# Three warm-up products moved behind the modulation, and all engine orders of an adaLN block replaced by another plan

## The chip, the core and the metric

The kernel runs on one core of a Trainium2 chip. The metric is device time in microseconds (us). Before the change the runs gave 277.48 us in the median (277.21 to 277.81, three runs).

## The reference

One transformer block with adaptive layer norm, on 2048 tokens of width D = 448. A vector c gives six modulation vectors. The first half is causal attention over a sliding window of 256 tokens with 16 heads of width 28, the second a gated MLP whose gate mixes tokens by a 2048 x 2048 matrix.

```python
mod = (silu(c) @ w_mod).reshape(1, 6, 1, 448)
sa, ca, ga, sb, cb, gb = mod[:, 0], ..., mod[:, 5]
h = layernorm(x) * (1 + ca) + sa
x = x + ga * (window_attention(h @ wqkv) @ wo)
h = layernorm(x) * (1 + cb) + sb
z = gelu(h @ w_in)                     # 448 -> 2 * 896
z2 = layernorm(z[..., 896:])
g = w_sp @ z2 + b_sp                   # over the tokens
x = x + gb * ((z[..., :896] * g) @ w_out)
```

## The kernel before

**Order.** The kernel writes down 1180 operations, each with what it depends on; an operation is a short group of instructions on one engine. Which engine executes an operation that could go to several (a copy out of PSUM, a normalisation), in what order each engine takes its operations, and which PSUM bank or buffer each one uses is all read from one string, `PLAN`, at the top of the file. An entry `p71.0` is operation 71, on TensorE, in bank or buffer 0; the letters p, d, a, t, s stand for TensorE (PE), VectorE (DVE), ScalarE (ACT), GpSimd (POOL) and SyncE (SP, which issues most DMAs). A program derives the semaphore waits from the dependencies and from that order. Each engine, and SP's queue, takes its operations strictly in the order of the plan.

**Stages, with the lines that the prediction names.**

- Start. `wmodA` (the part of `w_mod` for sa and ca), `wq_st`, `wv` and x are loaded. 37 warm-up products of a constant tile (L513, made at L566, called fillers) keep PE busy: 27 are meant for the time ahead of the modulation, ten for the gaps behind it. c is transposed (L516), silu applied (L519), and four operations of eight narrow products (L547) make sa and ca from `wmodA`. Four token tiles are transposed on PE (L750) and modulated on the way out of PSUM (L759, L761) into `hT`, the transposed h.
- Attention works in blocks of 512 tokens, in tiles of 128. `WQK` holds the q and k weights with each head padded to 32 rows (L619, L620). Products give K (L836, copied out to `KT` at L848 and L849), q (L812 for the first block, L778 for the others; copied to `qT` at L787, L788, L817) and V (L856, copied to `Vaug` at L860, L861). Scores: L941 for the first tiles, L971 (48 matmuls for half a tile), and L982 for a narrow rest that uses `QBD`, a block diagonal copy of q (cleared at L523, filled at L806, L830). Then the exponential on ACT (L927), the causal and window mask by a multiplication on DVE (L990, L1010), the product with V (L1017), the division by the row sums (L1031, L1033), a DMA that transposes the result (L466), the product with `wo_g` (L1043), and the sum with x on DVE (L1047). `wo_g` is `wo` scaled by ga (`gg_sb`), in four pieces (L603).
- The layer norms of the later blocks take statistics on DVE (L634, L637), a small addition (L641), a power on POOL (L643), a product (L659), and the normalisation (L654, or L661 with the mean folded in); then a DMA transposes the tile into `hT` (L466), and `hT` is modulated in four pieces a block (L740 on ACT, L742 on DVE or POOL; L1066, L1068 in the second half).
- The MLP: products with `w_in` for z2 (L1141, two token tiles a group) and z1 (L1162, transposed, four pieces a group), gelu on ACT (L1148 and L1170), the norm of z2 (L634 to L643, then L1153 on DVE). When all 16 tiles of z2 are normalised, the spatial product begins: 28 products of 16 matmuls (L1186), each followed by the addition of b_sp on DVE (L1190), the product with z1 on POOL (L1193) and, four token tiles at a time, the product with `w_out_g` (L1205), the last sum (L1215) and the way out (L1220).

The `lock` attributes at several operations are not used when the kernel is built.

Of the kernel before, what the change touches and what calls it, by code (L numbers as in the profile page):

```python
# [12 lines left out]
s2 d21 t25 t0 d22 t26 s4 s6 a1 p44.0 t27 t30 d109 p45.0 d107 d108 s8 s11 p46.0 p47.0 p48.0 p49.0 p50.0 p51.0  # L13
d110 s10 d111 a3 a5 a9 t31 t28 p52.0 p35.0 p53.0 p54.0 a7 t112 t32 d113.0 p55.0 p56.0 p57.0 p58.0 p59.0 p60.0
p61.0 p62.0 p63.0 p64.0 d114.1 p65.0 p66.0 p67.0 p68.0 p69.0 p70.0 t29 a36 t23 a100 t99 t34 p40.0 p41.1 s12
p42 p43 d82 p71.0 p123.2 p126.3 p72.2 p73.2 p74.2 p75.2 p76.2 p77.2 d81 p78.2 d127 d124 t24 d128 p138.0 t101
a102 t106 a125 a37 d117 d115 d118 d116 a103 d104 p139 a140 p147.2 p148 t105 d119 p135.3 p136 p79.2 p80.2 d179
p150.0 d175 d177 s14 a149 t120 d121.0 p151 d122.1 a137 p371.0 d181 p132.1 p129.6 d180 p141.7 a152 p142 d182
d176 d178 d183 t33 t184 d133 p144.0 p145 a372.0 t190 d130 d134 a146 d131 p153.6 d185.0 s192 d242 p377.0 d373
t186 t187.1 s193 d188 d143 d189.2 p154 p156.1 p157 s194 d375 d158 a378.1 d244 t191.3 p396.0 d379 s195 p162.0  # L20
d381 d39 d246 p163 d164 a155 d167 p169.7 p170 d166 p374.0 a397.2 a398 p376 p380 p382 d84 p403.0 a171 p92.1 p93
d94 s15 d401 d383 p172.7 p173 a404.1 d399 p89.0 p90 d91 a405 d406 a174 a165 p424.0 d243 d384.0 t83 p85.1 a168
p86 t197 t98 d88 d408 d199 p159.7 p160 t97 p400.0 s385 d198 d87 a425.0.0 p402 p407 a161 d240 s820 p431.0
p426.0 d245 p409 a196 p203.1 a432.2 d428 p204 p200.0 p201 a205 a427 p450.0 d410 d202 p216.1 a451.1.1 p217
p206.0 p207 d241 d411.1 a208 p429.0 p457.0 p430 p228.0 d247 t248 t249 t251 t253 a218 p229 p209.1 p210 d433
d250.0 p434 a458.3 s13 p476.0 d305 t255 d454 s257 a38 p435 d254.1 d230 d211 p225.0 p226 t95 a477.0.2 d215
# [225 lines left out]
def bass_adaLN_cond__sliding_block__mixer_gmlp__prompt_kernel(  # L252
# [290 lines left out]
    t_mA = []  # L543
# [17 lines left out]
    fillers = []  # L561
# [726 lines left out]
```

## Time and profile before

| | before |
|---|---|
| median of three runs | 277.48 us |
| the profiled execution | 277.41 us |
| its span on the core | 275.7 us |
| PE, DVE, ACT, POOL busy | 97%, 60%, 46%, 42% |
| granted PE clock in the span | 1.0 |
| DMA | 25.54 MB, 93 GB/s in the mean |

The span is the time from the first to the last instruction of the profiled execution; 1.7 us lie around it. Engines' busy shares are means over the span: DVE and ACT are close to full until about 110 us and idle for most of the rest, when PE does the spatial product. In a row of the timeline stand the start in us, the duration in us, the engine, line and operation, the output and inputs, the count of instructions, and in brackets how long the engine had been idle and whose result ended that. A row with a count covers instructions that overlap, so that its duration is not the sum of its parts.

### The profile page before, as it was taken

To read this page: it belongs to the slowest core of one execution; us is meant where nothing else is said; L and a number is where in the kernel's file an instruction comes from. 1 tells how busy PE (TensorE), PEld (TensorE's weight loads), DVE (VectorE), ACT (ScalarE), POOL (GpSimd) and SP (SyncE) were. 2 spreads that over 40 slices of the span, in tenths; PEclk is the share of its full clock that TensorE was granted. 3 is DMA by queue.
4 is the path that set the end of the run, shared out by engine and by line. 5 is a ranking of instruction groups with operands and counts; after the bars stand their busy time and mean duration, and the time that the engine had idled before them with its cause. 6 is when DMAs were issued, how large, how long until landed. Compare 5 with 4: busy or idle time off the path is not lost.

```text
span 275.7 us, 8403 instructions
## 1 busy us (share of the span) xinstructions
PE 267.6 (97%) x3742; PEld 153.4 (56%) x3752; DVE 164.1 (60%) x358; ACT 127.6 (46%) x152; POOL 114.6 (42%) x163
## 2 busy tenths in 40 slices
PE   8999879999999999999999999999999999999995
PEld 6887656767677775544544444444444544444452
DVE  3799899799889999987889200202302050236234
ACT  2689979988989988478876500000000000000000
POOL 7644472123139765816476100308807063106330
PEclk9999999999999999999999999999999999999999
DMA  7998423856316674768899998000000000002013
GB/s 208 312 225 127 120 60 45 162 97 114 22 33 166 99 80 61 98 133 144 207 172 162 230 178 178 0 0 0 2 0 0 11 2 0 0 23 86 0 50 100
DMA packets 66821, 25.54 MB, mean 93 GB/s; under 512 B 58465, under 2 KB 65698, under 8 KB 66786
## 3 DMA queue, kind: packets, MB, share of 16 engines
q1 hardware_dynamic: 65792, 23.98, 46.0%
q10 hardware_dynamic: 994, 1.03, 1.4%
q8 instruction: 29, 0.48, 0.8%
q14 instruction: 6, 0.05, 0.1%
HBM read 9.01 MB, written 1.84 MB: 39 GB/s over the span
## 4 chain that ended last, share of the span: by engine, by line
PE 85%; ACT 6%; DVE 5%; issue 2%; POOL 1%; DVEq 0%
PE ps L1186 35%; PE ps L1141 8%; PE ps L1205 8%; PE ps L1162 8%; PE ps L1017 5%; PE ps L971 4%; PE ps L836 4%; PE ps L1043 4%; PE ps L778 3%; PE ps L856 3%; ACT PW L927 3%; PE ps L513 2%; DVE PT L990 1%; ACT PT L927 1%; PE ps L812 1%
## 5 line engine op out<-in xcount | busy, mean ns | idle before, releaser
L1193 POOL TENSOR_TENSOR z1T<-tmpg,z1T 128x512 bf16<-128x512 bf16 x28 | 31.8, 1153 | 75.7 <-DVE tmpg L1190 75.6
L927 ACT ACTIVATE PW<-ps 128x2048 bf16<-128x2048 f32 (+1 forms) x42 | 59.9, 1450 | 5.5 <-PE ps L971 3.5
L1190 DVE TENSOR_TENSOR tmpg<-ps,bsp_bc 128x512 bf16<-128x512 f32 x28 | 19.0, 690 | 70.1 <-PE ps L1186 59.6
L1186 PE MATMUL ps<-wspB,z 128*128 128x512 bf16 x219 | 48.7, 379 | 0.3
L1186 PE MATMUL ps<-wspA,z 128*128 128x512 bf16 x219 | 48.6, 379 | 0.4 <-issue 0.2
L643 POOL TENSOR_TENSOR rs_all<-ve_all,neghalf 128x1 f32<-128x1 f32 (+2 forms) x37 | 25.9, 713 | 35.8 <-DVE ve_all L641 35.0
L1186 PEld LDWEIGHTS ps<-wspA,z 128*128 128x128 bf16 x224 | 21.8, 98 | 26.6 <-issue 0.4
L1186 PEld LDWEIGHTS ps<-wspB,z 128*128 128x128 bf16 x224 | 21.9, 98 | 26.1
L990 DVE TENSOR_TENSOR PT<-PW,mask 128x2048 bf16<-128x2048 bf16 x28 | 33.9, 1223 | 0.0
L1017 PE MATMUL ps<-Vaug,PT 128*128 128x32 bf16 x496 | 23.9, 177 | 0.1
L1017 PEld LDWEIGHTS ps<-Vaug,PT 128*128 128x128 bf16 x496 | 21.6, 96 | 3.2 <-DVE o_sb L1033 0.7
L1215 DVE TENSOR_TENSOR fin<-ps,x_sb 128x448 bf16<-128x448 f32 (+2 forms) x17 | 9.7, 593 | 21.1 <-PE ps L1205 21.0
L1141 PE MATMUL ps<-w_in,hT 64*128 64x448 bf16 x224 | 22.2, 350 | 0.0
L1205 PE MATMUL ps<-w_out_g,z1T 128*128 128x448 bf16 (+2 forms) x119 | 22.2, 342 | 0.0
L1162 PE MATMUL ps<-hT,w_in 64*128 64x512 bf16 x196 | 22.0, 376 | 0.0
L634 DVE BATCH_NORM_STATS2 st_all<-x_sb 128x6 f32<-128x448 bf16 x32 | 19.1, 614 | 2.6 <-DMA x_sb<-in_A_x_dram 2.6
L1017 PE MATMUL ps<-Vaug,PW 128*128 128x32 bf16 x224 | 20.3, 176 | 0.0
L634 DVE BATCH_NORM_STATS2 st_all<-z 128x6 f32<-128x448 bf16 x32 | 18.5, 608 | 3.0 <-ACT z L1148 2.8
L1148 ACT ACTIVATE z<-ps 128x896 bf16<-128x896 f32 x16 | 14.0, 912 | 10.2 <-PE ps L1141 10.2
L1017 PEld LDWEIGHTS ps<-Vaug,PW 128*128 128x128 bf16 x224 | 17.7, 96 | 1.1
L971 PEld LDWEIGHTS ps<-qT,KT 32*128 32x128 bf16 (+1 forms) x1344 | 13.6, 90 | 7.8 <-ACT PW L927 4.9
L971 PE MATMUL ps<-qT,KT 32*128 32x128 bf16 (+5 forms) x1344 | 17.4, 197 | 0.3 <-issue 0.2
(105 smaller groups left out, 359.4 us busy)
## 6 DMA issues: line engine op xcount, KB each, us to landing
out_dram<-fin SPq DMA_DIRECT2D x15, 112.0 KB, 1.7
wmodB<-in_w_mod_dram SPq DMA_DIRECT2D x1, 1568.0 KB, 15.9
x_sb<-in_A_x_dram SPq DMA_DIRECT2D x3, 448.0 KB, 8.6
w_in<-in_B_w_in_dram SPq DMA_DIRECT2D x3, 448.0 KB, 4.9
w_out_g<-in_B_w_out_dram SPq DMA_DIRECT2D x1, 784.0 KB, 4.9
bsp_bc<-in_B_b_sp_dram SPq DMA_DIRECT2D x1, 512.0 KB, 5.3
hT<-xn SPq DMA_TRANSPOSE x28, 3.0
w_in<-in_B_w_in_dram SPq DMA_DIRECT2D x2, 224.0 KB, 5.0
```

Source lines behind the costliest of these rows:

```text
L634: st = [dve(0.62 if True else 0, lambda e, t=t, ci=ci, s=s: e.bn_stats(st_all[:, slot, t, ci, :], s()), deps(t), prio) for ci, s in enumer ...
L643: return pool(0.4 + 0.15 * len(tiles), lambda e: e.tensor_tensor(rs_all[:, slot, a:b], ve_all[:, slot, a:b], neghalf[:, 0:b - a], ALU.pow) ...
L927: ex = act(xdur, lambda e, out_ap=out_ap, in_ap=in_ap: e.activation(out_ap(), in_ap(), ACT.Exp, scale=SCALE), [s] + list(after), v - 8.0 + ...
L971: fm.append(lambda e, hm=hm, qi=qi, key=key, kn=kn, lo=lo, hi=hi, col=col, p0=p0, t=t, j=j: e.matmul(ps[p0:p0 + kn, hm.slot[t], col:col + ...
L990: mk_both = lock_d(1.2, lambda e, hp=hp, at_w=at_w, pad=pad, f0=f0: e.tensor_tensor(cols(hp.slot[0] * 2048, [[256, 8], [128, 2], [1, 128]] ...
L1017: fns.append(lambda e, hp=hp, hO=hO, hi=hi, bi=bi, kb=kb, hd=hd, nb=nb, a=at[hi][bi], p_of=p_of: e.matmul(ps[:, hO.slot[0], 32 * hd:32 * h ...
L1141: return lambda e, kc, p0, start, stop: e.matmul(ps[:, hs[t % 2].slot[hf], 0:D], lhsT=hT[p0:p0 + 64, kc, t * 128:(t + 1) * 128], rhs=w_in[ ...
L1162: return lambda e, kc, p0, start, stop: e.matmul(ps[:, hs[b // 2].slot[b % 2], :], lhsT=w_in[p0:p0 + 64, kc, ft * 128:(ft + 1) * 128], rhs ...
L1186: m = pe(16 * MMS, [lambda e, h=h, si=si, ft=ft, tb=tb: e.matmul(ps[:, h.slot[0], :], lhsT=z2[:, si, ft * 128:(ft + 1) * 128], rhs=(wspA i ...
L1190: a = dve(0.7, lambda e, h=h, ht=ht, tb=tb: e.tensor_tensor(tmpg[:, ht.slot[0], :], ps[:, h.slot[0], :], bsp_bc[:, tb * 512:(tb + 1) * 512 ...
L1193: u = pool(1.16, lambda e, ht=ht, ft=ft, tb=tb: e.tensor_tensor(z1T[tb][:, ft, :], tmpg[:, ht.slot[0], :], z1T[tb][:, ft, :], ALU.mult), [ ...
L1205: return [lambda e, ft=ft: e.matmul(ps[:, h.slot[0], 0:hi - lo], lhsT=z1T[t // 4][:, ft, (t % 4) * 128:(t % 4 + 1) * 128], rhs=w_out_g[:, ...
```

## The change

The string `PLAN` is replaced whole, and two lines that state the place of the fillers (they are read when a plan is made, not when the kernel is built) go from 27 to 24 fillers ahead of the modulation. No operation is added or taken out; 87 go to another engine and nearly all to another place in their queue. In the new file line numbers are lower by one.

```diff
-    t_mA[0].after = fillers[26:27]
-    fillers[27].after = t_mA
+    t_mA[0].after = fillers[23:24]
+    fillers[24].after = t_mA
...
-p42 p43 d82 p71.0 p123.2 p126.3 p72.2 p73.2 p74.2 p75.2 p76.2 p77.2 d81 p78.2 d127 d124 t24 d128 p138.0 t101
...
```

On PE there are now 9 + 15 fillers ahead of the four modulation operations, and the 13 behind them stand singly or up to four at a time between the transposes and the K products, where before ten stood, eight of them ahead of the K products and two behind. On ACT the second clearing of `QBD` (L523) moves from a place behind the fourth exponential of 2048 columns, at 36 us, to a place between the first and the second K copy. On SP the load of the third block of x goes ahead of the DMA transposes of the second block, and the load of `wo` behind them.

POOL, where it works on the second and third block of the first half. Before (`wmodE` is a small rearrangement of weights, `ve_all`, `rs_all` and `xn` belong to the layer norm):

```order
L742 TENSOR_SCALAR hT<-hT,modT 112x512
L603 TENSOR_TENSOR wo_g<-wo_g,gg_sb 112x448 x2
L641 TENSOR_SCALAR ve_all<-mv_all 128x4
L643 TENSOR_TENSOR rs_all<-ve_all,neghalf 128x4
L659 TENSOR_SCALAR ve_all<-mv_all,rs_all 128x1 x3
L603 TENSOR_TENSOR wo_g<-wo_g,gg_sb 112x448
L661 TENSOR_SCALAR xn<-x_sb,rs_all,ve_all 128x4x112
L603 TENSOR_TENSOR wo_g<-wo_g,gg_sb 112x448
L661 TENSOR_SCALAR xn<-x_sb,rs_all,ve_all 128x4x112
L742 TENSOR_SCALAR hT<-hT,modT 112x512
```

POOL at the same place in the program now, beginning with the same modulation of the second block:

```order
L741 TENSOR_SCALAR hT<-hT,modT 112x512
L640 TENSOR_SCALAR ve_all<-mv_all 128x4
L642 TENSOR_TENSOR rs_all<-ve_all,neghalf 128x4
L658 TENSOR_SCALAR ve_all<-mv_all,rs_all 128x1
L660 TENSOR_SCALAR xn<-x_sb,rs_all,ve_all 128x4x112
L602 TENSOR_TENSOR wo_g<-wo_g,gg_sb 112x448
L660 TENSOR_SCALAR xn<-x_sb,rs_all,ve_all 128x4x112 x2
L741 TENSOR_SCALAR hT<-hT,modT 112x512 x2
L602 TENSOR_TENSOR wo_g<-wo_g,gg_sb 112x448 x2
```

Two of the four scalings of `wo_g` stood ahead of the third block's `ve_all`; now one has gone to DVE, one stands between the normalisations, and two behind the modulations of the third block. A third normalisation (L660) of that block has come over from DVE. On DVE the statistics of this block have moved ahead of a mask step, and on PE the V product that waited at 39 us has moved behind seventeen other operations.

ACT, at the passage to the MLP. Before (the last exponential, then gelus of z2 tiles, `z_82`, of z1 pieces, `z1T`, and modulations of `hT` for the second block):

```order
L927 ACTIVATE PW<-ps 128x8x64
L1148 ACT_TABLE_LOAD
L1148 ACTIVATE z_82<-ps 128x896 x3
L1066 ACTIVATE hT<-hT,modT 128x512
L1148 ACTIVATE z_82<-ps 128x896
L1170 ACTIVATE z1T_75<-ps 128x512 x4
L1148 ACTIVATE z_82<-ps 128x896 x4
L1066 ACTIVATE hT<-hT,modT 128x512 x4
```

ACT at the same passage now:

```order
L926 ACTIVATE PW<-ps 128x8x64
L1147 ACT_TABLE_LOAD
L1147 ACTIVATE z_82<-ps 128x896 x2
L1169 ACTIVATE z1T_75<-ps 128x512 x4
L1065 ACTIVATE hT<-hT,modT 128x512 x2
L1147 ACTIVATE z_82<-ps 128x896 x4
L1169 ACTIVATE z1T_76<-ps 128x512
```

The four z1 gelus and two modulations (one of them came from POOL) now stand ahead of the third and fourth z2 gelu. PE has the same change: the first z1 group (L1162) goes ahead of the second z2 group (L1141), and the group for tiles 6 and 7 ahead of that for tiles 4 and 5.

DVE, ahead of the spatial product. Before (`st_all` and `mv_all` are statistics of z2, `z_82<-z_82,mv_all,rs_all` its normalisation, `tmpg` the first step behind the spatial product):

```order
L634 BN_STATS st_all<-z_82 128x6 x2
L637 BN_AGGR mv_all<-st_all 128x2
L1153 TENSOR_SCALAR z_82<-z_82,mv_all,rs_all 128x896
L641 TENSOR_SCALAR ve_all<-mv_all 128x1
L634 BN_STATS st_all<-z_82 128x6
L641 TENSOR_SCALAR ve_all<-mv_all 128x1
L1153 TENSOR_SCALAR z_82<-z_82,mv_all,rs_all 128x896 x2
L634 BN_STATS st_all<-z_82 128x6
L1153 TENSOR_SCALAR z_82<-z_82,mv_all,rs_all 128x896
L637 BN_AGGR mv_all<-st_all 128x2
L1153 TENSOR_SCALAR z_82<-z_82,mv_all,rs_all 128x896 x5
L1190 TENSOR_TENSOR tmpg<-ps,bsp_bc 128x512 x13
```

DVE ahead of the spatial product now:

```order
L1152 TENSOR_SCALAR z_82<-z_82,mv_all,rs_all 128x896 x2
L633 BN_STATS st_all<-z_82 128x6
L1152 TENSOR_SCALAR z_82<-z_82,mv_all,rs_all 128x896
L633 BN_STATS st_all<-z_82 128x6
L636 BN_AGGR mv_all<-st_all 128x2 x2
L1152 TENSOR_SCALAR z_82<-z_82,mv_all,rs_all 128x896
L640 TENSOR_SCALAR ve_all<-mv_all 128x1
L1152 TENSOR_SCALAR z_82<-z_82,mv_all,rs_all 128x896 x4
L640 TENSOR_SCALAR ve_all<-mv_all 128x1
L1152 TENSOR_SCALAR z_82<-z_82,mv_all,rs_all 128x896 x5
L1189 TENSOR_TENSOR tmpg<-ps,bsp_bc 128x512 x10
```

Thirteen normalisations now stand behind the statistics of the tile last but one, where before there were nine; four of them are of tiles whose statistics are long done.

More of the change, by code (lines that the diff above doesn't have):

```diff
@@ L18 @@
[L18 to L26, printed above, removed]
-p222.1 p223 t252.2 s258 d213 d214 p452.0 a227 p483.0 d436 d437.0 p455.0 a453 d224 p219.0 p456 d480 a484.2 p220
```

114 lines of the change are left out of this document (62 added, 52 removed).

## The prediction

> **What bounds the kernel now.** I read the page's busy times and its chain that ended last, then the busy times by stage, then the timeline of one engine after another at the places where TensorE (PE) stands still. The rows below are from the page and from the view of busy times by stage; behind the stage stand its length, then busy us and instruction count of PE, weight loads, VectorE (DVE), ScalarE (ACT) and GpSimd (POOL), the clock, the DMA share and GB/s.
>
> ```profile
> PE 267.6 (97%) x3742; PEld 153.4 (56%) x3752; DVE 164.1 (60%) x358; ACT 127.6 (46%) x152; POOL 114.6 (42%) x163
> PE 85%; ACT 6%; DVE 5%; issue 2%; POOL 1%; DVEq 0%
> 25.00:42.00 17.00, 14.60 (x432) 10.88 (x429) 15.45 (x30) 14.81 (x16) 9.93 (x12) 1.00 0.41 79
> 42.00:88.00 46.00, 45.96 (x1308) 32.56 (x1307) 41.92 (x82) 43.03 (x44) 14.85 (x22) 1.00 0.51 94
> 88.00:105.00 17.00, 16.62 (x532) 12.08 (x532) 16.37 (x32) 16.07 (x17) 12.51 (x14) 1.00 0.65 80
> 105.00:154.50 49.50, 49.44 (x582) 24.72 (x580) 43.27 (x116) 35.66 (x53) 26.80 (x53) 1.00 0.84 147
> ```
>
> PE is the bound: 97% of the span, and the change takes no product away. So the most that an order can win is the time in which PE stands still or runs slowly. In 25 to 42 us that is 2.4 us of 17; in the three stages behind it 0.04, 0.38 and 0.06. Behind 154.5 us stands the spatial product, back to back, with the same work in both kernels. All that can be won lies ahead of 42 us, and all of it must then be carried through 42 to 105 us, where DVE and ACT are themselves 91 to 96% busy.
>
> **The start (three fillers, one more early ACT step).** PE's timeline, the sequencer's row that issues the load of `wv`, that load's time to landing, and three ACT rows (one of them from 36 us):
>
> ```profile
> 3.31 4.02 PE L513 MATMUL ps<-fill 128*128 128x256 bf16 x18
> 7.13 1.27 PE L547 MATMUL ps<-sc_sb,wmodA 112*128 112x64 bf16 x32
> 8.79 0.93 PE L513 MATMUL ps<-fill 128*128 128x256 bf16 x7
> 9.86 2.11 PE L836 MATMUL ps<-hT,WQK 112*128 112x128 bf16 x32
> 13.22 0.92 PE L856 MATMUL ps<-wv,hT 112*128 112x448 bf16 x4
> 3.63 0.58 SPq L393 DMA_DIRECT2D wv<-in_A_wqkv_dram  x1
> DMA to landing us min/median/max: 9.5/9.5/9.5
> 13.05 0.60 ACT L817 ACTIVATE qT<-ps 128x512 bf16<-128x512 f32 x1 [0.26 <-PE ps L812]
> 14.18 0.54 ACT L860 ACTIVATE Vaug<-ps 128x448 bf16<-128x448 f32 x1 [0.53 <-PE ps L856]
> 36.05 1.07 ACT L523 ACTIVATE QBD<-zero 128x1024 f32<-128x1024 f32 x1
> ```
>
> A filler ahead of the modulation takes 4.02/18 = 0.22 us, one behind it 0.93/7 = 0.13 us. Three fewer ahead let the modulation (L547) begin 0.65 us sooner, at about 6.5. That is ahead of the place where the fillers changed pace, so some of its 32 matmuls run at the slow pace; half of the 0.65 goes there, and about 0.3 us is left. The fillers in between the K products (L836) use up most of that, and then the first V product (L856) stops it: `wv` lands at 3.63 + 9.5 = 13.13 us, and the product began at 13.22. **I take 0** for the start; the bounds are -0.3 (all of it kept) and, if the slow pace lasts longer, the price of the last rival below.
>
> The clearing of the second half of `QBD` (L523, 1.07 us) moves from 36.05 to ahead of ACT's second K copy, at about 11.7. Behind it the K and the q copy end some 0.2 us later than in the row at 13.05, but still ahead of the V copy, which waits for PE until 14.18. At 36 us ACT then has 1.07 us more. I take 0, with bounds 0 and +0.4.
>
> The Trainium skill ("TensorE: Matmul & The Clock Gate", Part 1) says that PE gets full clock after a busy window of about 3.4 us and that the window runs free of the kernel. The trace agrees so far: 0.22 against 0.13 us for a filler. By that rule the modulation's own matmuls keep the window as busy as fillers do, and the sum stays as it is; only a window judged idle would bring the last rival.
>
> **25 to 30 us.** Two POOL scalings of `wo_g` (L603) leave this place, one for DVE and one for a place some ten steps later on POOL.
>
> ```profile
> 25.07 0.46 DVE L1010 TENSOR_TENSOR PT<-PT,mask 128x512 bf16<-128x512 bf16 x1
> 26.12 1.28 DVE L1010 TENSOR_TENSOR PT<-PT,mask 128x512 bf16<-128x512 bf16 x1
> 27.32 1.45 DVE L742 TENSOR_SCALAR hT<-hT,modT 112x512 bf16<-112x512 bf16 x2
> 26.08 2.22 POOL L603 TENSOR_TENSOR wo_g<-wo_g,gg_sb 112x448 bf16<-112x448 bf16 x2 [0.82 <-DMA wo_g<-in_A_wo_dram]
> 28.95 1.89 PE L778 MATMUL ps<-hT,WQK 112*128 112x512 bf16 x8 [0.72 <-ACT hT L740]
> ```
>
> The same mask step took 0.46 us alone and 1.28 beside the scalings. With them gone, DVE gets to the modulations of `hT` (L742) 0.8 us sooner, and PE waited 0.72 us for the last of these. The new order also puts three of the four modulations on DVE in a row, so not all of it is won: **-0.6 us**, bounds -0.72 and 0.
>
> **30 to 39 us.** The pieces at 32.34, 33.53 and 34.61 are from the chain in order of time, the row with three durations (least, median, most, in ns) from the groups of L661, the others from the timelines:
>
> ```profile
> 32.34 1.12 POOL ve_all L641
> 33.53 1.05 POOL rs_all L643
> 34.61 0.40 DVE xn L654
> 35.46 1.21 DVE L990 TENSOR_TENSOR PT<-PW,mask 128x2048 bf16<-128x2048 bf16 x1
> 36.58 1.81 DVE L661 TENSOR_SCALAR xn<-x_sb,rs_all,ve_all 128x448 bf16<-128x448 bf16 x1
> L661 DVE TENSOR_SCALAR xn<-x_sb,rs_all,ve_all x9: 361/393/1811, 18.4 to 128.2; 128x448 bf16<-128x448 bf16 x9
> 38.32 0.67 DVE L849 CAST KT<-ps 128x512 bf16<-128x512 f32 x1
> 35.48 2.08 POOL L603 TENSOR_TENSOR wo_g<-wo_g,gg_sb 112x448 bf16<-112x448 bf16 x1
> 38.23 1.05 POOL L603 TENSOR_TENSOR wo_g<-wo_g,gg_sb 112x448 bf16<-112x448 bf16 x1
> 39.05 0.93 PE L856 MATMUL ps<-wv,hT 112*128 112x448 bf16 x4 [1.55 <-DVE KT L849]
> ```
>
> This is the one long halt of PE, 1.55 us. It waits for a K copy that stands on DVE behind L661, which took 1.81 us where its median is 0.39: 1.4 us too long, beside a scaling that itself took 2.08 where another took 1.05. Behind that lies a chain over POOL (the two small steps at 32.34 and 33.53) that held DVE until 34.61. The change undoes this three times over: the scaling at 35.48 goes behind POOL's `hT` modulations of the third block, L661 here moves to POOL, where its kind takes 0.71 us, the statistics come ahead of the mask step, so that the POOL chain starts about a mask step (1.2 us) sooner, and this V product goes seventeen steps later on PE. Any one of them covers 1.2 to 1.4 of the 1.55 us. **-1.5 us**, bounds -1.55 and 0 (the halt comes back at another product). Next late is ACT's exponential, which is one pass after the other there.
>
> The Trainium skill ("SBUF — State Buffer", the section on SBUF's two separate sides) calls the port pair of VectorE and GpSimd an exclusive lock: whichever instruction starts first holds it to its end. The trace agrees within 0.2 us: the scaling at 35.48 would be held by the mask step until 36.67 and end at 37.72 (traced: 37.56), and L661 ends 0.4 to 0.8 us after that. By that rule moved scalings are held again wherever they meet a mask step, which speaks against the change and is the mechanism of the first rival.
>
> **42 to 105 us.** The cover for what was moved here is DVE's 46 - 41.92 = 4.1 us, then 17 - 16.37 = 0.6 us. One scaling on DVE (a two-input step of 128x448 takes 0.6 to 0.7 us by the row at 38.32, nearest in size) and three on POOL fit the first stage. I carry the 2.1 us through at no loss; bounds 0 and +2.1.
>
> **105 to 154 us.** Here the order on PE changes: the z1 products (L1162) come ahead of the second z2 group (L1141), and two `hT` modulations (L1066) now stand on ACT between the gelus.
>
> ```profile
> 115.13 1.73 ACT L1148 ACTIVATE z<-ps 128x896 bf16<-128x896 f32 x2 [1.16 <-PE ps L1141]
> 118.72 2.06 ACT L1170 ACTIVATE z1T<-ps 128x512 bf16<-128x512 f32 x4 [0.22 <-PE ps L1162]
> 126.80 1.51 ACT L1066 ACTIVATE hT<-hT,modT 128x512 bf16<-128x512 bf16 x2
> 115.49 3.19 PE L1162 MATMUL ps<-hT,w_in 64*128 64x512 bf16 x28
> 120.25 3.96 PE L1141 MATMUL ps<-w_in,hT 64*128 64x448 bf16 x40
> ```
>
> In before's times: the z1 block ends 2.56 us sooner than now, at about 116.1, its first two gelus may start near 115.45. Then ACT has 2.06 + 1.51 + 1.73 = 5.3 us to do, to 120.75, before PE may enter the third z2 group, for which it is ready at 120.25. **+0.5 us**, bounds 0 and +0.9 (the same again at the group for the third block).
>
> **Sum:** 0 + 0 - 0.6 - 1.5 + 0 + 0.5 = -1.6. The profiled execution took 277.41 us (span 275.7 and 1.7 around it), the median of the runs is 277.48; so **275.8 us**.
>
> **Rivals.** *The lead is given back in 42 to 105 us.* DVE is 96% busy in 88 to 105 us, and the L1010 row shows 0.8 us lost when a POOL step meets it. Three meetings cost DVE 2.4 us, more than the lead. The work on PE would allow it, DVE wouldn't: 277.4. For it: 0.6 us to spare. Against it: 4.1 us to spare ahead of that.
>
> *Slower: the z2 normalisations (L1153) pile up ahead of the spatial product*, whose first matmul waits for all 16 of them.
>
> ```profile
> 147.02 1.14 DVE L634 BATCH_NORM_STATS2 st_all<-z 128x6 f32<-128x448 bf16 x2
> 151.26 2.32 DVE L1153 TENSOR_SCALAR z<-z,mv_all,rs_all 128x896 bf16<-128x896 bf16 x5
> 144.85 1.73 ACT L1148 ACTIVATE z<-ps 128x896 bf16<-128x896 f32 x2 [0.43 <-PE ps L1141]
> 154.60 3.62 PE L1186 MATMUL ps<-wspA,z 128*128 128x512 bf16 x16 [0.16 <-issue]
> ```
>
> Now DVE needs 151.26 + 2.32 - 147.02 = 6.56 us from the statistics at 147.02 to its last normalisation, with nine of them in it. The new order has thirteen: four more at 2.32/5 = 0.46 make 8.4 us. Its earliest start is the first gelu's end, 144.85 + 1.73/2 = 145.7, which gives 154.1, and PE is ready at about 154.4. So it decides from 0.3 us of delay on DVE. At the delay of now (147.02, that is 1.3 us) PE waits to 155.4: +1.0 us, and without the lead 278.4.
>
> *All of it holds:* the start's 0.3, none of the 0.5, and the 0.38 us of 88 to 105 us: 277.41 - 2.1 - 0.3 - 0.4 = 274.6.
>
> *The slow pace lasts.* If the fillers' early end lets PE run on slowly for another stretch as long as the one at 3.31 (4 us), half of that is lost, +2.0 with the other terms unchanged: 277.8. Against it: PE has work without a gap there.
>
> **Chances.** Forecast 0.45 (275.0 to 276.6), lead given back 0.17, normalisations 0.20, all holds 0.12, slow pace 0.06. 0.2% is 0.55 us, about what a measurement can tell here. Faster: 0.45 + 0.12 and 0.05 of the second; within 0.2%: 0.10 of the second and 0.03 of the last; slower: the rest, 0.25. The range takes in the bounds of the 30 to 39 us term and the slower rival, and leaves out what is below 274.4 and above 278.6.
>
> **What would show it.** Right: no PE halt of over 0.5 us between 28 and 42 us; L661 on DVE at its 0.39 us throughout; PE some 2 us ahead at 64 and at 105 us; a PE wait of about 0.5 us on ACT between 117 and 121 us; the first spatial matmul near 153.0. Wrong: a new wait for DVE's K or q copies, mask steps (L990) well over 1.21 us, or a PE wait on L1153 ahead of the spatial product. What would upset the whole is a loss behind 154.5 us, where I count none.

## The result, and the profile after

The changed kernel takes 281.41 us in the median (279.92 to 282.87, four runs) against 277.64 (277.21 to 278.11) for the kernel before on the same chip: a ratio of 1.0134 with an interval of 1.0094 to 1.0174, so it is slower. The prediction was 275.8 us. The profiled execution took 279.92 us with a span of 278.2 us, 2.5 more than before. The ratios and the counts by clock below leave out slow runs (five single runs of the edited kernels, of 280.90 to 1485.64 us), while the medians are of all runs.

The page's busy times and the chain that ended last, after the change:

```profile
PE 267.4 (96%) x3752; PEld 153.6 (55%) x3752; DVE 165.2 (59%) x357; ACT 127.4 (46%) x152; POOL 114.0 (41%) x164
PE 79%; DVE 9%; DMA 3%; ACT 3%; POOL 2%; issue 2%; SPq 1%
```

PE does the same work and is still the bound, but its part of the chain fell from 85% to 79%. The busy times by stage (columns as in the prediction) show where PE stood still:

```profile
25.00:42.00 17.00, 15.59 (x468) 11.23 (x457) 15.91 (x34) 15.10 (x18) 7.93 (x9) 1.00 0.57 107
42.00:88.00 46.00, 45.11 (x1289) 32.74 (x1288) 41.57 (x73) 42.29 (x41) 16.25 (x22) 1.00 0.49 77
88.00:105.00 17.00, 15.35 (x525) 11.70 (x523) 15.08 (x32) 14.61 (x17) 6.80 (x11) 1.00 0.76 122
105.00:154.50 49.50, 48.29 (x581) 24.59 (x579) 44.55 (x118) 34.82 (x49) 30.93 (x59) 1.00 0.80 138
```

Between 25 and 42 us PE gained 1.0 us (14.60 before). It lost 0.85, 1.27 and 1.15 us in the three stages behind that, which had been almost without a gap. Now the timeline of the changed kernel: PE where it stood still (and the q product, which stood still before and doesn't now, and the first spatial product), then DVE, POOL and SP beside these places. `<-issue` in a bracket means that the profile shows nothing that the engine waited for.

```profile
13.37 0.93 PE L855 MATMUL ps<-wv,hT 112*128 112x448 bf16 x4 [0.41 <-DMA wv<-in_A_wqkv_dram]
28.52 0.81 PE L777 MATMUL ps<-hT,WQK 112*128 112x512 bf16 x3
37.12 0.19 PE L1016 MATMUL ps<-Vaug,PT 128*128 128x32 bf16 x1 [1.11 <-DVE PT L989]
45.34 0.21 PE L970 MATMUL ps<-qT,KT 32*32 32x64 bf16 x8 [0.82 <-issue]
91.15 0.18 PE L1016 MATMUL ps<-Vaug,PT 128*128 128x32 bf16 x1 [1.60 <-issue]
110.56 2.25 PE L1140 MATMUL ps<-w_in,hT 64*128 64x448 bf16 x22 [1.14 <-POOL hT L1067]
156.90 0.82 PE L1185 MATMUL ps<-wspA,z 128*128 128x512 bf16 x3
33.09 0.68 DVE L787 CAST qT<-ps 128x512 bf16<-128x512 f32 x1
33.93 1.48 DVE L805 COPY QBD<-qT 32x512 bf16<-32x512 bf16 x2
35.44 1.63 DVE L989 TENSOR_TENSOR PT<-PW,mask 128x2048 bf16<-128x2048 bf16 x1
34.21 1.04 POOL L602 TENSOR_TENSOR wo_g<-wo_g,gg_sb 112x448 bf16<-112x448 bf16 x1 [1.57 <-DMA wo_g<-in_A_wo_dram]
35.24 2.54 POOL L660 TENSOR_SCALAR xn<-x_sb,rs_all,ve_all 128x448 bf16<-128x448 bf16 x2
107.72 1.29 POOL L666 COPY xn<-xn 128x64 bf16<-128x64 bf16 x1
108.99 1.52 POOL L1067 TENSOR_SCALAR hT<-hT,modT 128x512 bf16<-128x512 bf16 x2
84.51 1.30 SPq L465 DMA_TRANSPOSE wspA<-in_B_w_sp_dram  x1
87.73 3.02 SPq L465 DMA_TRANSPOSE wspA<-in_B_w_sp_dram  x1
```

The two waits on which the prediction rested are gone: the q product at 28.52 us has no bracket (0.72 before), and the V product that waited 1.55 us doesn't either. In their place stand four new halts. Their brackets give the balance: -0.72 - 1.55 + 1.11 + 0.82 + 1.60 + 1.14 = +2.40 us, against 156.90 - 154.60 = 2.30 us at the first spatial product and 2.5 us in the span. Behind it the two kernels run alike. One of the four, the 0.82 us, seems to belong to this execution: none of the traces of the eight edits of the changed kernel below has it. The places of the other three halt in other traces too.

That leaves the medians: the profiled execution is the fastest of the four. Two runs, of 279.92 and 280.70 us, had a mean granted clock of 1.0; the two of 282.13 and 282.87 us had 0.988. This second part of the loss is told below under the clock.

### The profile page after: what moved, and what is told of

Same layout as the page of the kernel before. It is cut to its first block, busy times and chain, and to the rows that moved or that the text cites. A ratio compares the mean times of both kernels' runs of the same rounds, so it can differ in the third digit from the quotient of the medians.

```text
span 278.2 us, 8410 instructions
## 1 busy us (share of the span) xinstructions
PE 267.4 (96%) x3752; PEld 153.6 (55%) x3752; DVE 165.2 (59%) x357; ACT 127.4 (46%) x152; POOL 114.0 (41%) x164
## 4 chain that ended last, share of the span: by engine, by line
PE 79%; DVE 9%; DMA 3%; ACT 3%; POOL 2%; issue 2%; SPq 1%
PE ps L1185 35%; PE ps L1140 8%; PE ps L1204 8%; PE ps L1161 8%; PE ps L1016 4%; DMA wv<-in_A_wqkv_dram 3%; PE ps L970 3%; DVE PT L989 3%; PE ps L855 3%; PE ps L835 3%; PE ps L1042 3%; PE ps L777 2%; ACT PW L926 2%; DVE st_all L633 1%; PE ps L811 1%
## 5 line engine op out<-in xcount | busy, mean ns | idle before, releaser
L1185 PE MATMUL ps<-wspB,z 128*128 128x512 bf16 x224 | 49.7, 379 | 0.0
L1185 PE MATMUL ps<-wspA,z 128*128 128x512 bf16 x224 | 49.3, 379 | 0.0
L989 DVE TENSOR_TENSOR PT<-PW,mask 128x2048 bf16<-128x2048 bf16 x28 | 35.5, 1276 | 0.1
L1016 PE MATMUL ps<-Vaug,PT 128*128 128x32 bf16 x496 | 25.1, 177 | 2.8 <-issue 1.6
L1016 PEld LDWEIGHTS ps<-Vaug,PT 128*128 128x128 bf16 x496 | 22.3, 96 | 4.3 <-DVE PT L989 2.1
L835 PE MATMUL ps<-hT,WQK 112*128 112x128 bf16 x256 | 17.9, 219 | 0.5 <-ACT hT L758 0.5
```

What stands on the lines that cost most here:

```text
L835: km = lambda g, kc, start, stop, h=h, t=t: lambda e: e.matmul(ps[:, h.slot[0], g * 128:(g + 1) * 128], lhsT=WQK[0:CP, kc, 16 + 4 * g:20 + ...
L989: mk_both = lock_d(1.2, lambda e, hp=hp, at_w=at_w, pad=pad, f0=f0: e.tensor_tensor(cols(hp.slot[0] * 2048, [[256, 8], [128, 2], [1, 128]] ...
L1016: fns.append(lambda e, hp=hp, hO=hO, hi=hi, bi=bi, kb=kb, hd=hd, nb=nb, a=at[hi][bi], p_of=p_of: e.matmul(ps[:, hO.slot[0], 32 * hd:32 * h ...
L1185: m = pe(16 * MMS, [lambda e, h=h, si=si, ft=ft, tb=tb: e.matmul(ps[:, h.slot[0], :], lhsT=z2[:, si, ft * 128:(ft + 1) * 128], rhs=(wspA i ...
```

## The experiments

Four theories stood against each other. *Order at 33 to 41 us*: VectorE has the mask step too late. *Code*: the halt at 89.5 to 91.15 us is PE waiting for its own instructions, because two loads of `wspA` on SP now stand there. *POOL*: the halt at 110 us comes from modulations queued behind other steps. *Fillers and clock*: with fewer fillers PE gets its full clock late or loses it. The rival to all of these is that DVE and ACT are simply full, so that a halt taken away comes back. Edits are shown as the order of the engine that they change; ratios are to the kernel before, on the same chip.

| run | median us | ratio | interval | runs at clock 1.0 / below |
|---|---|---|---|---|
| before_24_fillers | 278.47 | 0.9990 | 0.9958 to 1.0022 | 6 / 4 |
| after_27_fillers | 280.60 | 1.0081 | 1.0047 to 1.0115 | 7 / 4 |
| after_wsp_loads_later | 279.58 | 1.0046 | 1.0018 to 1.0074 | 10 / 2 |
| before_wsp_early | 280.88 | 1.0093 | 1.0058 to 1.0128 | 1 / 9 |
| after_hT_first | 280.11 | 1.0097 | 1.0064 to 1.0130 | 3 / 3 |
| after_mask_first | 281.31 | 1.0146 | 1.0105 to 1.0186 | 3 / 3 |
| after_stats_later | 281.60 | 1.0112 | 1.0069 to 1.0154 | 0 / 6 |
| after_three_undone | 279.09 | 1.0045 | 1.0016 to 1.0074 | 8 / 4 |
| after_four_undone | 279.59 | 1.0034 | 1.0003 to 1.0065 | 5 / 6 |
| after_q_on_ACT | 278.51 | 1.0029 | 0.9999 to 1.0059 | 10 / 1 |
| before_scalings_later | 277.86 | 0.9984 | 0.9955 to 1.0012 | 9 / 2 |
| before_K_copy_first | 276.98 | 0.9973 | 0.9951 to 0.9995 | 12 / 0 |
| before_K_q_first | 277.32 | 0.9959 | 0.9932 to 0.9986 | 6 / 6 |
| before_L661_on_POOL | 276.69 | 0.9968 | 0.9944 to 0.9993 | 12 / 0 |

"Clock 1.0" stands for a mean clock of 0.998 or more. The kernel before itself had 59 runs beside these at clock 1.0, with medians of 277.50 to 277.67 us on each of four chips, and 46 below it, with medians of 277.87 to 278.81 us. The rows of the table come from these four chips, and two ratios whose intervals overlap can't be told apart.

### The fillers

The part that the change is named after, put alone into the kernel before, and taken back out of the changed kernel:

```diff
 PE of before_24_fillers, against before
-L513 MATMUL ps<-fill 128x256 x18
+L513 MATMUL ps<-fill 128x256 x15
 L547 MATMUL ps<-sc_sb,wmodA
...
-L513 MATMUL ps<-fill 128x256 x7
+L513 MATMUL ps<-fill 128x256 x10
 L836 MATMUL ps<-hT,WQK
 PE of after_27_fillers, against after
-L512 MATMUL ps<-fill 128x256 x15
+L512 MATMUL ps<-fill 128x256 x18
 L546 MATMUL ps<-sc_sb,wmodA
```

> The kernel before with nothing changed but the place of three fillers: 24 ahead of the modulation, ten of them in one row behind the first transposes. Clock theory (the four runs of the changed kernel lie at 279.9, 280.7 with a mean granted clock of 1.0 and at 282.1, 282.9 with 0.988, so the earlier end of the fillers lets PE lose the full clock for a time in some runs): some runs show a clock below 1.0 and are about 2 us longer, the median 277.5 to 279.5. Order theory (the clock difference belongs to the chip or to other parts of the new order): all runs at clock 1.0 and 277.2 to 278.0.

> The changed kernel with 27 fillers ahead of the modulation again, everything else as changed. Clock theory: all runs at clock 1.0, 279.5 to 280.7, the spread of 3 us gone. Order theory: runs with and without the lower clock as in the changed kernel, median 280 to 282.

The three fillers do nothing that can be told: 0.9990 with an interval that holds 1, and with 27 of them the changed kernel is still slower by 0.8%. Runs below full clock came in both, 4 of 10 and 4 of 11, and on the same chip in 16 of 33 runs of the kernel before, so the clock theory fell too. What little the start can win can be lost to `wv`: PE waited 0.41 us for that load in the row at 13.37 us above, and 0.3 to 0.9 us in most traces, with 24 fillers or 27. The loss must come from the orders.

### The loads of `wspA`

Two loads went behind the transposes that they stood among:

```diff
 SP of after_wsp_loads_later, against after
-L465 DMA_TRANSPOSE wspA<-in_B_w_sp_dram 128x1024
 L432 DMA w_in<-in_B_w_in_dram 128x1792
 L465 DMA_TRANSPOSE hT<-o_sb 128x4x128
-L465 DMA_TRANSPOSE wspA<-in_B_w_sp_dram 128x1024
...
+L465 DMA_TRANSPOSE wspA<-in_B_w_sp_dram 128x1024 x2
```

> The changed kernel with two transposing loads of the spatial weight, which now stand on SP at 84 and 88 us, behind the last transposes of attention at about 113 us, where the kernel before has them later still. Fetch theory (PE's halt of 1.6 us at 89.4 us, for which no dependency is seen, waits for its own code: the 16 KB load of instructions that began at 87.19 took 2.52 us instead of 0.9 to 1.6, because the DMA engines were full of those loads and a 448 KB load): the halt is gone, that instruction load takes under 1.7 us, and the span falls by 1.0 to 1.8 us. Rival (the halt is PE's own, or another load is to blame): the halt stays within 0.3 us and the time within 0.5 us.

The ratio fell from 1.0134 to 1.0046, on another chip; after_27_fillers, on the same chip as this run, has 1.0081, and the two intervals overlap. So the median gained between 1.0 and 2.4 us, and the trace says more. The same PE row, in the timeline of this run:

```profile
90.15 0.18 PE L1016 MATMUL ps<-Vaug,PT 128*128 128x32 bf16 x1 [0.23 <-issue]
```

The view of the DMA queues from 87 to 91 us has one instruction load in both kernels (packets, MB, share of 16 engines' time). In the changed kernel:

```profile
q8 instruction: 1, 0.02, 3.9%
```

and with the loads later:

```profile
q8 instruction: 1, 0.02, 1.4%
```

A share of 16 engines over 4 us, that is of 64 us: 2.5 us against 0.9 us for the same piece of code. In the DMA records of the nine traces of the changed kernel and its edits that load took 2.52, 2.37, 2.34 and 2.29 us with the `wspA` loads beside it and 0.88, 0.94, 0.94 and 0.89 without; in the fifth trace with them, after_stats_later, it took only 1.49 us but began late, 0.98 us ahead of PE's stop where the other eight began 2.1 to 2.6 us ahead, and the halt was 1.88 us. PE stopped each time at the same instruction, in the middle of a group of twelve that has no wait inside it, and went on 1.36 to 1.57 us behind the end of the load: the halts were 1.05 to 1.88 us long in the five traces with the loads there and 0.23 in the four without. So this halt is PE's wait for code, and the loads of `wspA` beside it make the code late.

A count of PE's instructions in the traces (weight loads, products, semaphore steps) says the same. There is one load of code for some 260 instructions (29 loads for some 7540). In these nine traces every halt of over 0.25 us with `<-issue` stands 192 or 193 instructions over a multiple of 256: number 4288 is the one above in all nine, 1729 the 0.82 us at 45.34 us, and two in other traces are 705 and 4801 (after_hT_first, then after_mask_first):

```profile
25.79 0.19 PE L970 MATMUL ps<-qT,KT 32*32 32x32 bf16 x3 [1.04 <-issue]
100.82 0.19 PE L1016 MATMUL ps<-Vaug,PT 128*128 128x32 bf16 x1 [1.26 <-issue]
```

The halts at 37.12 and 110.56 us, which wait for DVE and POOL, are numbers 1260 and 5436, that is 236 and 60 over. So the 0.82 us stands at a boundary of code too. How code comes late isn't always its load: PE went on 1.27 us behind the end of the last load at 705, but 1.92 at 1729 and 2.46 at 4801. Most such halts come and go from one trace to the next; only the one at 4288 stood in all nine.

The opposite was tried too: the kernel before with SP's order of the change between 84 and 91 us.

```diff
 SP of before_wsp_early, against before
+L466 DMA_TRANSPOSE wspA<-in_B_w_sp_dram 128x1024
+L433 DMA w_in<-in_B_w_in_dram 128x1792
+L466 DMA_TRANSPOSE hT<-o_sb 128x4x128
+L466 DMA_TRANSPOSE wspA<-in_B_w_sp_dram 128x1024
+L466 DMA_TRANSPOSE hT<-o_sb 128x4x128
 L466 DMA_TRANSPOSE hT<-xn_90 128x4x128 x3
...
-L466 DMA_TRANSPOSE wspA<-in_B_w_sp_dram 128x1024 x2
```

> The kernel before with the SP queue of the changed kernel at 84 to 91 us: one load of the spatial weight, a 448 KB load of w_in and a second load of the spatial weight around the transpose at 86.4. Fetch theory (a burst of loads there slows the load of PE's own instructions): the instruction load that begins near 86 us takes over 2 us instead of 1.67, PE halts for 0.5 to 1.8 us with no dependency in sight, the time rises by 0.5 to 2 us and more runs show a clock below 1.0. Rival (the halt in the changed kernel had to do with its PE order): no halt over 0.4 us there, within 0.4 us of before.

It is slower by 0.9%, but not by the mechanism that this run was made for: the instruction load near 86 us took 1.01 us, not over 2, and PE has no `<-issue` halt there. Its timeline, SP and PE:

```profile
88.83 1.31 SPq L466 DMA_TRANSPOSE wspA<-in_B_w_sp_dram  x1
90.19 1.27 SPq L466 DMA_TRANSPOSE hT<-o_sb  x1
94.50 0.92 PE L1043 MATMUL ps<-wo_g,hT 112*128 112x448 bf16 x4 [2.19 <-DMA hT<-o_sb]
```

Here the product with `wo_g` waits for a transpose that SP issued only at 90.19 us, behind the second load of `wspA`. It is a plain wait on a queue. The run shows that such a load has a price on SP as well; for the wait for code the nine traces above are the evidence, not this one.

### POOL ahead of the MLP

```diff
 POOL of after_hT_first, against after
-L1067 TENSOR_SCALAR hT<-hT,modT 128x512
+L1067 TENSOR_SCALAR hT<-hT,modT 128x512 x3
 L660 TENSOR_SCALAR xn_90<-x_sb,rs_all,ve_all 128x448
...
 L666 COPY xn_90<-xn_90 128x64
-L1067 TENSOR_SCALAR hT<-hT,modT 128x512 x2
```

> The changed kernel with one move on POOL: two modulations of hT (L1067) that ran at 108.99 and 109.74 go to right behind the one at 96.54, ahead of the normalisations of the next block. Halt theory (PE's halt of 1.3 us ahead of the first product with w_in, at 109.2 to 110.6, waits for these two, which stand on POOL behind 4.5 us of other steps though their transposed input had landed by 98): the halt falls under 0.4 us and the time by 0.9 to 1.4 us, to 279.9 to 280.5. Rival (the normalisations now come late and their transposes hold the second group back): the same time is lost at the third z2 group at 122 us, within 0.5 us of the changed kernel.

The wait of 1.14 us at 110.56 us is gone: PE has no halt between 105 and 130 us in this run. The ratio went from 1.0134 to 1.0097, some 1.0 us, with intervals that overlap. In the row at 107.72 us above POOL can be seen to finish a copy of `xn` first; with the order turned round, PE waits for nothing there.

### The halt at 37 us

First the mask step went ahead of the copies into `QBD`; then, apart from that, three statistics went out of DVE's way.

```diff
 DVE of after_mask_first, against after
-L658 TENSOR_SCALAR ve_all<-mv_all,rs_all 128x1
-L805 COPY QBD<-qT 32x512 x2
 L989 TENSOR_TENSOR PT<-PW,mask_60 128x2048
-L805 COPY QBD<-qT 32x512
+L658 TENSOR_SCALAR ve_all<-mv_all,rs_all 128x1
+L805 COPY QBD<-qT 32x512 x3
 DVE of after_stats_later, against after
-L633 BN_STATS st_all<-x_sb 128x6 x2
 L653 TENSOR_SCALAR xn<-x_sb,mv_all,rs_all 128x4x112
...
 L989 TENSOR_TENSOR PT<-PW,mask_60 128x2048 x2
+L633 BN_STATS st_all<-x_sb 128x6 x3
```

> The changed kernel with one move on DVE: the mask step that PE waited for at 37 us (the one at 35.44 that took 1.63) goes ahead of the three copies into QBD. Halt theory (PE's halt of 1.1 us at 36 to 37.1 comes from the mask step standing behind 1.5 us of copies, and the copies' users are not late): the halt falls under 0.4 us, the time by 0.8 to 1.3 us to 280.0 to 280.6, and fewer runs show a mean clock below 1.0. Rival (DVE is full there, the same time is lost at the copies' users or at the next mask step): within 0.5 us of the changed kernel.

> The changed kernel with four steps moved on DVE: three statistics of the third block of x (L633 at 31.74, 32.27, 37.19) and a small one behind them go behind the mask step at 40.33, which is still earlier than in the kernel before. Load theory (PE's halts at 37 and 40 us come from 1.8 us of DVE work that the new order pulled in here from 45 to 53 us, while DVE has no room; moving the mask step alone only moved the halt to the next mask step): both halts together fall from 1.6 us to under 0.6, the time by 0.8 to 1.5 us to 279.9 to 280.6. Rival (the statistics fill gaps of DVE here and something else bounds): within 0.5 us of the changed kernel.

Neither took the loss away: the halt was gone in the first and 1.66 us long in the second. With the mask first, PE stood still at two other places; its timeline:

```profile
39.44 0.39 PE L981 MATMUL ps<-QBD,KT 128*128 128x256 bf16 x2 [0.35 <-DVE QBD L805]
41.52 0.19 PE L1016 MATMUL ps<-Vaug,PT 128*128 128x32 bf16 x1 [1.31 <-DVE PT L989]
```

With the statistics later, DVE first stood idle and was then late all the same:

```profile
33.15 0.69 DVE L787 CAST qT<-ps 128x512 bf16<-128x512 f32 x1 [0.96 <-PE ps L777]
33.99 2.04 DVE L805 COPY QBD<-qT 32x512 bf16<-32x512 bf16 x2
36.06 1.62 DVE L989 TENSOR_TENSOR PT<-PW,mask 128x2048 bf16<-128x2048 bf16 x1
```

So the load on DVE was not the cause, and the theory that the statistics delay the mask fell. The rows of the changed kernel at 33 to 37 us show part of the lateness: beside POOL's L602 and L660 two `QBD` copies took 1.48 us, where one clear of POOL takes 0.28, and the mask 1.63 us, where 1.21 was usual, some 1.3 us in all. No run moved these POOL steps away. What was tested is the order: the q copy, which the change moved from ACT to DVE, waits for a product, and `QBD` copies and the mask stand behind it. The last run on this takes the q copy back to ACT and puts the mask ahead, both at once. Between these stand two sums of the edits so far: after_three_undone has mask, hT and `wspA`; after_four_undone has statistics, hT and `wspA`. after_q_on_ACT adds to the latter:

```diff
 DVE and ACT of after_q_on_ACT
-L787 CAST qT<-ps 128x512
+L989 TENSOR_TENSOR PT<-PW,mask_60 128x2048
 L658 TENSOR_SCALAR ve_all<-mv_all,rs_all 128x1
+L805 COPY QBD<-qT 32x512 x4
...
 L926 ACTIVATE PW<-ps 128x4x512
-L786 ACTIVATE qT<-ps 128x512
+L786 ACTIVATE qT<-ps 128x512 x2
```

> The changed kernel with three moves together: the mask step ahead of the QBD copies, the two hT modulations early on POOL, the two loads of the spatial weight behind the attention. If these three halts are the loss and add up (1.1 + 1.3 + 1.6 us in the profiled run): 276.9 to 277.9 and nearly all runs at a mean clock of 1.0. If the new orders lose the time elsewhere as soon as a halt is filled: 279 to 280.

> The changed kernel with the statistics later, the two hT modulations early on POOL, and the two loads of the spatial weight behind the attention. If the halts at 37 to 40, 89 and 109 us are the whole loss: 276.8 to 278.0, nearly all runs at a mean clock of 1.0, no halt of PE over 0.9 us between 15 and 154 us. If the new orders lose time elsewhere too (steps on ACT and DVE that wait on each other between 42 and 105 us): 278.3 to 279.3.

> The changed kernel with the four undone steps (statistics later, hT first, wspA loads later) and two more at 33 to 37 us: the q copy at 33.48 us goes from VectorE back to ScalarE, and the mask step of the product that waited at 37.67 us goes ahead of the copies into QBD. If the order on VectorE holds that product (mask behind q copy and QBD copies, where VectorE first idles 0.81 us for the q product), the halt of 1.3 to 1.6 us at 36.2 to 37.7 goes, and the time falls by 1.0 to 1.6 us to 278.2 us or below, a ratio of 0.997 to 1.001. If VectorE and ScalarE are simply full there, a halt of about the same size comes back within 5 us at another mask step or QBD product, and the ratio stays at 1.003.

The two sums bring the ratio to 1.0045 and 1.0034, that is from 3.8 us of loss to about 1. Neither comes down to the time that was named for the halts as the whole loss (277.9 and 278.0 us at most): a halt for a mask step is left in both, 1.31 us at 41.37 us and 1.26 us at 37.67 us. The last run takes that halt away; PE's timeline has these waits from 20 to 60 us, and no other above 0.25 us:

```profile
22.86 0.92 PE L595 MATMUL ps<-wmodB,sc_rep 112*128 112x448 bf16 x4 [1.51 <-DMA wmodB<-in_w_mod_dram]
36.08 1.07 PE L835 MATMUL ps<-hT,WQK 112*128 112x128 bf16 x16 [0.37 <-ACT qT L786]
55.85 0.73 PE L855 MATMUL ps<-wv,hT 112*128 112x448 bf16 x3 [0.95 <-issue]
```

So the order theory holds for the halt, though the run doesn't show which of the two moves did it. In the time it can't be seen: 1.0029 against 1.0034, on different chips, where 1.001 at most was expected. This profiled execution was the slowest but one of its runs (280.39 us). It waited 0.8 us longer than after_four_undone for `wmodB` (there 0.70 us), was level with it again at 50 us (the same scores begin at 50.50 us here and at 50.44 there), and then stood 0.95 us at a boundary of code (number 2240), 1.50 us behind the end of an instruction load, and 0.63 us at another at 104.85 us. Of the halt's 1.3 us only the trace tells.

### The old halt at 39 us, by itself

Four edits of the kernel before, each against the halt that the prediction valued at 1.5 us: scalings behind the normalisations, the K copy ahead of L661, the K and the q copy ahead of it, and L661 on POOL.

```diff
 POOL of before_scalings_later
-L603 TENSOR_TENSOR wo_g<-wo_g,gg_sb 112x448
-L661 TENSOR_SCALAR xn<-x_sb,rs_all,ve_all 128x4x112
-L603 TENSOR_TENSOR wo_g<-wo_g,gg_sb 112x448
-L661 TENSOR_SCALAR xn<-x_sb,rs_all,ve_all 128x4x112
+L661 TENSOR_SCALAR xn<-x_sb,rs_all,ve_all 128x4x112 x2
+L603 TENSOR_TENSOR wo_g<-wo_g,gg_sb 112x448 x2
 DVE of before_K_copy_first
+L849 CAST KT<-ps 128x4x128
 L661 TENSOR_SCALAR xn<-x_sb,rs_all,ve_all 128x4x112
-L849 CAST KT<-ps 128x4x128
 L788 CAST qT<-ps 128x512
 DVE of before_K_q_first
+L849 CAST KT<-ps 128x4x128
+L788 CAST qT<-ps 128x512
 L661 TENSOR_SCALAR xn<-x_sb,rs_all,ve_all 128x4x112
 POOL of before_L661_on_POOL (the same row taken out of DVE)
 L659 TENSOR_SCALAR ve_all<-mv_all,rs_all 128x1 x3
+L661 TENSOR_SCALAR xn<-x_sb,rs_all,ve_all 128x4x112
 L603 TENSOR_TENSOR wo_g<-wo_g,gg_sb 112x448
```

> The kernel before with the two scalings of wo_g that stand on POOL at 35.5 and 38.2 us moved behind the block's normalisations. Theory of the forecast (L661 on DVE at 36.58 is held 1.4 us by the scaling beside it, and PE's halt of 1.55 us at 39 us follows from that): L661 falls from 1.81 to under 1.0 us, the halt to under 0.9 us, and 0.7 to 1.4 us are won: 276.1 to 276.9. Rival (the POOL normalisation that comes to stand there holds DVE as well, or the lead is given back later): within 0.5 us of before.

> The kernel before with one move on DVE: the K copy that PE waited for at 39 us goes ahead of L661, which is held by the scaling beside it. Halt theory with the clock (the halt of 1.55 us is the only long one of the kernel before, and the runs with a mean clock of 0.994 are those where a clock window with this halt in it was judged idle): the halt falls under 0.5 us, the time by 1.0 to 1.5 us to 276.2 to 276.8, and all runs show a clock of 1.0. Rival (the held L661 only moves the wait to the q copy behind it, or DVE loses it again before 64 us): within 0.5 us of before; clock rival (the low clock has nothing to do with PE's halts): as many runs at 0.994 as in the kernel before.

> The kernel before with the K copy and the q copy behind it both ahead of L661 on DVE. Behind the K copy alone PE still halted 1.3 us at 39.0 for the q copy. Halt theory: that halt falls under 0.5 us and 0.4 to 1.0 us more are won, 276.0 to 276.6, all runs at a clock of 1.0. Rival (DVE is full here as well, so that the copies into QBD or the mask step behind L661 come later by as much): as with the K copy alone, 276.8 to 277.3.

> The kernel before with one step of the change alone: the normalisation L661 that held VectorE for 1.81 us goes to GpSimd, ahead of the scaling that it collided with. By the prediction's own step this one move covers 1.2 to 1.4 us of the halt of 1.55 us: 276.1 to 276.4 us at full clock, ratio 0.994 to 0.996. If the halt only moves on to the q copy, the QBD copies or o_sb, as in the two runs with early copies, a halt of 0.8 us or more stands behind it before 43 us and the ratio is 0.997 to 1.000; and if GpSimd's later steps then hold the transposes of the third block, PE waits for hT between 43 and 48 us.

With the scalings later, DVE and POOL read:

```profile
35.71 0.39 DVE L661 TENSOR_SCALAR xn<-x_sb,rs_all,ve_all 128x448 bf16<-128x448 bf16 x1
37.33 2.40 DVE L806 COPY QBD<-qT 32x512 bf16<-32x512 bf16 x3
37.19 2.08 POOL L603 TENSOR_TENSOR wo_g<-wo_g,gg_sb 112x448 bf16<-112x448 bf16 x2
40.74 0.19 PE L1017 MATMUL ps<-Vaug,PT 128*128 128x32 bf16 x1 [1.40 <-DVE o_sb L1033]
```

L661 takes its 0.39 us, as the prediction said. But the scalings now meet the three `QBD` copies, which took 1.14 us before and take 2.40, and PE loses 1.40 us at `o_sb` in place of 1.55. With the K copy first, 0.79 us are left for the q copy and 0.62 come at `o_sb`; with K and q first, 1.58 us come at `o_sb`, behind `QBD` copies of 2.06 us. The move of L661 to POOL, a part of the change taken by itself, shows the same in its timeline:

```profile
35.79 1.75 POOL L661 TENSOR_SCALAR xn<-x_sb,rs_all,ve_all 128x448 bf16<-128x448 bf16 x1
38.19 2.29 DVE L806 COPY QBD<-qT 32x512 bf16<-32x512 bf16 x3
41.48 0.19 PE L1017 MATMUL ps<-Vaug,PT 128*128 128x32 bf16 x1 [1.27 <-DVE o_sb L1033]
```

At full clock it takes 276.69 us against 277.51, so 0.8 of the 1.55 us are won: between "the halt goes" and "it comes back", though by the sign named for it, a halt of 0.8 us or more ahead of 43 us, it came back. The others won 0.2 us (scalings later), 0.5 (K copy) and 0.6 (K and q copy) at full clock. In none of the four did the halt shrink as far as its theory said. All three of K copy, K and q copy, and L661 on POOL beat the kernel before, by 0.3 to 0.4%, and their intervals overlap.

### The clock

In the traces, half clock came behind long halts of PE. The busy times of after_27_fillers around two of them; the clock is the third number from the end:

```profile
35.30:38.70 3.40, 1.71 (x35) 1.25 (x33) 3.34 (x5) 2.83 (x4) 1.64 (x3) 1.00 0.68 78
38.70:42.11 3.41, 3.41 (x85) 3.01 (x82) 3.28 (x7) 1.96 (x2) 0.08 (x1) 0.50 0.43 83
89.90:93.30 3.40, 1.80 (x69) 1.29 (x69) 1.89 (x5) 3.40 (x5) 2.99 (x6) 1.00 1.11 161
93.32:96.73 3.41, 3.41 (x94) 2.10 (x92) 3.20 (x6) 1.19 (x2) 0.00 (x0) 0.50 0.96 146
```

A stretch in which PE was busy for about half the time, because of one halt of 1.6 to 1.7 us, is followed by 3.41 us at half clock, full of work. From the end of the first such stretch to the start of the second are 51.2 us, 15 times 3.41: the clock goes by windows of that length. Two half-clock windows make a mean clock of 0.988, one makes 0.994. There are eight in all in the traces (the others in before_24_fillers, before_wsp_early, after_hT_first and after_stats_later), each behind a window in which halts of 1.44 to 2.19 us left PE busy for 1.24 to 2.03 us.

No window with 2.10 us or more, from 9 us on, was followed by half clock. The halt of 1.55 us in the kernel before fell across two windows in its profiled execution, and the clock stayed. The first row is the later of these windows; the second, from after_q_on_ACT, is the one exception below 2.03 us:

```profile
37.90:41.31 3.41, 2.26 (x46) 1.69 (x46) 3.25 (x8) 1.98 (x3) 2.08 (x3) 1.00 0.37 73
19.75:23.16 3.41, 1.90 (x32) 1.53 (x29) 2.51 (x7) 2.48 (x3) 0.41 (x1) 1.00 1.56 165
```

So busy time in a window isn't the whole rule; what else counts stays open. The kernel before ran below full clock in 46 of 105 runs, and then took about 1.1 us more on three of four chips (278.60 against 277.53, 278.65 against 277.50, 278.81 against 277.67) and 0.35 us on the fourth. How many runs of a kernel fell below follows the longest halt of its one profiled execution only at the ends: none of 12 at 0.79 us (before_K_copy_first), 15 of 16 at 1.88 and 2.19 us (after_stats_later, before_wsp_early). In between lies anything from none of 12 (before_L661_on_POOL, 1.27 us) to 6 of 11 (after_four_undone, 1.26 us); the halts of the runs without a profile aren't known.

The Trainium skill ("TensorE: Matmul & The Clock Gate", Part 1) says that the window is 3413 ns long and runs free of the kernel: the traces agree with 3.41 us and with a phase that differs from run to run. Its rule that PE's clock falls after an idle window, so that gaps up to about 3.4 us do no harm, doesn't hold here: gaps of 1.4 to 2.2 us were enough in eight windows.

## Why the prediction was wrong

In the profiled executions the prediction was 4.0 us off: a loss of 2.4 us instead of a gain of 1.6. Of these 4.0 us, 1.1 lie in 30 to 39 us, 2.4 in 42 to 105 us and 0.6 behind that; 25 to 30 us gave 0.1 more than forecast.

**The start, 0, and the clearing of `QBD`, 0.** Nothing speaks against the first: 0.9990 for the fillers alone (0.9958 to 1.0022, too wide to tell 0 from -0.3 us), and PE waits for `wv` as forecast. The second wasn't tested alone; no halt stands at its two places.

**25 to 30 us, -0.6.** Right: the wait of 0.72 us at the q product is gone.

**30 to 39 us, -1.5.** Wrong, and it went to the bound that the prediction had written down beside it: "the halt comes back at another product". Its reason, three remedies of which any one would do, counted only remedies. The halt is one place in a chain of steps on DVE; behind it stood `QBD` copies and masks with as little time to spare, and the new order put a q copy that waits for PE and two `QBD` copies ahead of a mask: 1.11 us at 37.12 us. On the way these steps met POOL's scaling and normalisations, at some 1.3 us for DVE. That is the mechanism of the first rival, only in this stage and not behind 42 us; how much of the halt is order and how much is this collision stays open. The four edits of the kernel before show the same without the change: 0.2 to 0.8 us are won at full clock, not 1.5, and 0.79 to 1.58 us of halt come back a few steps on. With the scalings later the collision moves to the `QBD` copies (1.14 to 2.40 us).

**42 to 105 us, 0 with a bound of +2.1.** This is the step that failed most: 0.82 + 1.60 = 2.4 us were lost. The first rival priced the stage by DVE and mask steps; neither halt is one of those. The one of 1.60 us is code that came late beside the moved loads of `wspA`. The prediction priced nothing of SP's new order in this stage. The 0.82 us stand at a boundary of code as well, among 48 products without a wait between them. Why that piece came late stays open: its load was of ordinary length (1.14 us) and ended 1.9 us ahead, and no other trace has this halt, so as far as these nine traces tell, that part is chance and not the change.

**105 to 154 us, +0.5.** Right in sign, too small. The wait on ACT between 117 and 121 us didn't come. What came is 1.14 us at 110.56 us, for two modulations that the new order left on POOL behind copies of `xn`; the prediction had looked at those on ACT only.

**The rivals.** That z2's normalisations pile up didn't happen: the page gives 0.4 us in all for the wait of the spatial product's weight loads on them, and none for its products. Of the chance of slower, 0.25, 0.20 stood on that mechanism, so it was right for a reason that wasn't there. The range ended at 278.6; the profiled run is at 279.92, and half of the runs lie above 282 us through the clock, of which the prediction had only the start in mind.

**Signs named ahead.** No halt of 0.5 us between 28 and 42 us: there was one of 1.11. L661 at 0.39 us on DVE: this step is now an L660 on POOL, where two of them took 2.54 us beside the mask. PE 2 us ahead at 64 us: not seen, since 1.11 + 0.82 of the 2.27 us won were lost by then. Of its signs of being wrong one came: the mask step at 35.44 us took 1.63 us, where 1.21 was the mark.

## What to carry to other kernels

A halt taken away from the bound engine is worth what the next step in the same queues leaves: walk the feeding engine's queue on from the removed wait, step by step, until one step has more time to spare than the halt was long. When a whole order is replaced, look at every queue that changed, the one that issues the loads and the small engines too, since a kernel at 97% has no gap that can hide a new wait. Before a halt is put down to a change, look whether it stands in a second trace. And ask of each halt longer than about 1.4 us whether it takes the clock with it.

## What the runs showed of the hardware

PE's code comes by DMA like the data: 29 pieces in a run, 0.48 MB together. A piece mostly took 0.9 to 1.4 us, the one at 88 us 2.3 to 2.5 us in four of five traces with two loads of `wspA` beside it, and PE went on 1.4 to 1.6 us behind its end. The Trainium skill ("Runtime: NRT & Kernel Launch", Instruction fetch mechanics) gives blocks of 16 KiB, which 0.48 MB over 29 agrees with, and calls the crossing mostly hidden; in this kernel, with groups of narrow products that follow each other every 0.02 to 0.03 us, one crossing cost 1.60 us.

Second, a window of 3.41 us with 1.4 us or more of halt in it was followed by half clock in eight of nine cases, so a halt of 1.6 us can cost 2.7 us. It matters where the halt falls in the window, which fits that the same kernel has two times 1.1 us apart.

Third, the collision of DVE and POOL lengthens copies as well as masks. The median `QBD` copy of the kernel before took 0.29 us; three in a row took 1.14 us there, where only the first met a POOL step, and 1.46 to 2.63 us in other traces beside POOL's scalings and normalisations.
